# Sets of many short matmuls are kept four microseconds apart in the list schedule

## The chip, the cores and the metric

The kernel runs on one core of one Trainium2 chip. The metric is the device time of one execution in microseconds. The core's engines work side by side, each in the order of its own instruction queue: TensorE (PE) multiplies matrices, VectorE (DVE) and ScalarE (ACT) work elementwise and empty the PE's result banks, GpSimd (POOL) and SyncE (SP) issue transfers. A weight load (PEld in the profile) stands before every matmul in the PE's queue.

## The reference

For 2048 tokens with 512 channels the output is `g * a + (1 - g) * b`, where `g` is a sigmoid of a dot product of the token with `gate_w`.

- `a` is a state-space layer. For each channel a kernel `K` of length 2048 is summed from 128 complex exponentials, `K = 2 * einsum("dn,dnl->dl", C, P).real` with `P = exp(A * dt * l)`; the tokens are convolved with it over time (in the reference by an FFT of length 4096) and `u * D_skip` is added.
- `b` is a gated product without a nonlinearity: `h = (x @ w_gate) * (x @ w_up)`, then `h @ w_down`, with 1792 hidden columns.

All of it is float32.

## The kernel before

**The gated product.** Tokens, weights and `h` are each split into a high and a low float32 part, and each product is three matmuls of 128x128 by 128x512 (`THREE`: low weight, low token, both high). The 1792 hidden columns are 14 tiles in five groups, the tokens four chunks of 512; `hidden` makes one tile of `pg` and `pu` (eight products), `down` adds `h` into the output tiles `y`. 672 such products make 2016 large matmuls. The split tokens `xhi` and `xlo` are written to DRAM once (`x_d`) and read again, tile by tile through SP's queue, at each change of chunk. Weights come as `raw<-in_wts`.

**The convolution.** The channels go in 16 blocks of 32 (`k_block`) and, for the transforms, in four quarters of four blocks. DVE and ACT build two tables of powers, `x` and `v`, for a block; the PE multiplies them (`kgen`, 64 short matmuls into one bank `k`), and ACT moves the bank into `kt`. After four blocks `k_first` does the first Fourier stage of the kernel in two sets (8 and 24 matmuls). `transforms` then does the second stage (`m_second`, four sets of 64 matmuls from `in`, `w2s`), the product of the spectra on DVE (`m_product`), the inverse stage (`m_inverse`, two sets of 64 matmuls from `y`, `w3s`) and the last stage (`m_last`, two sets of four larger matmuls). Between the stages the data go through DRAM: `sk_d` and `su_d` into `m_second`, `y_d` into `m_last`. The short matmuls are plain float32 and work in parts of the array (`tile_position`). Each stands in the profile as two weight loads and two MATMUL records, so that a set of 64 is 128 MATMUL records. In the profile a `k<-v,x` set is `kgen`, `k<-in,w2s` (in the last quarter `k<-v,w2s` and `k<-x,w2s`) is `m_second`, and `k<-y,w3s` is `m_inverse`.

**What sets the order.** Nothing is issued directly. Every piece of work is a task with an engine, a duration in microseconds, what it reads and writes, and a rank, given to `add`. `Work.run` is a list scheduler: at each step it takes, over all engines, the task that can start first by its own account of time (then the lower rank), and notes its end. A product of the gated part has rank 2 and the convolution's sets have rank 1, 0 or -1, so a set goes ahead of the products as soon as its inputs are there, and the products fill the PE in between. The order that comes out is issued engine by engine (`InOrder` holds each engine to it), so the chip keeps the order but not the scheduler's times. The scheduler knows the durations and the number of buffers; it knows nothing of how instructions reach an engine. A set and a product stand in it like this:

```
add("pe", 0.681, fn, r=[...], w=[pg], rank=2, after=after)     # product: three large matmuls
add("pe", 2.15, kgen, r=[x, v], w=[pk], rank=0, hold=[kt])     # set of 64 short ones
```

All instructions are recorded by the one line L100 of a helper, so the profile's groups are told apart by the names of their tiles.

## Time and profile before

| | us |
|---|---|
| median of 3 runs | 633.33 (632.41 to 633.38) |
| the profiled execution | 631.22 |
| its span, from the first to the last instruction | 629.4 |
| PE busy in the span | 608.8 (97%) |
| DVE, ACT, POOL busy | 486.1, 397.0, 106.1 |
| DMA: bytes moved, mean rate | 142.63 MB, 227 GB/s |

The span is the time between the first and the last instruction of the profiled execution; 1.8 us of its 631.22 us lie around it. A view that names "issue" as the end of an idle time means that the engine waited for nothing that the profile shows: no other engine and no transfer of the kernel. Matmuls start before the ones ahead of them have ended, and their ends are modelled, so the spacing of the starts tells more than the busy time: large matmuls follow each other at 0.227 us, though each is given as 0.39 us long.

### The profile page before, as it was taken

What the parts mean: (1) busy time and instruction counts of PE and PEld (TensorE: products, weight loads), DVE (VectorE), ACT (ScalarE), POOL (GpSimd) and SP (SyncE); (2) the same over time, 40 slices, a digit from 0 to 9 for tenths busy, and PEclk for the clock granted to TensorE, in tenths of its full rate; (3) what the DMA queues carried; (4) which work ended last, traced back from release to release, by engine and by line L of the source; (5) the groups of instructions that cost most, each with busy time, mean ns of one, the idle gap of its engine ahead of it and who ended that gap; (6) DMA issues with size and microseconds to landing.
All of it is one profiled execution on the core that took longest, in us unless ns stands there. A gap on an engine that the chain in (4) does not pass through costs nothing.

```text
span 629.4 us, 17934 instructions
## 1 busy us (share of the span) xinstructions
PE 608.8 (97%) x7526; PEld 469.1 (75%) x7526; DVE 486.1 (77%) x760; ACT 397.0 (63%) x903; POOL 106.1 (17%) x157
## 2 busy tenths in 40 slices
PE   7899999999999999999999999999999998999997
PEld 5667768688687787877777887778787676786885
DVE  6858999999999898999999999899853255632113
ACT  5379778968787764887977687796544542222220
POOL 3143332211021110202110101201010030102210
PEclk9999999999999999999999999999999999999999
DMA  8899868557879697969998398899889598958841
GB/s 310 266 338 334 298 191 317 180 164 238 231 184 284 179 240 224 223 200 257 196 321 219 93 247 264 210 222 275 242 239 326 171 245 215 280 152 193 161 68 67
DMA packets 111892, 142.63 MB, mean 227 GB/s; under 512 B 7876, under 2 KB 66756, under 8 KB 111556
## 3 DMA queue, kind: packets, MB, share of 16 engines
q1 hardware_dynamic: 90100, 105.05, 52.9%
q0 software_dynamic: 21568, 36.45, 28.1%
q8 instruction: 59, 0.97, 0.6%
q14 instruction: 21, 0.17, 0.1%
q10 hardware_dynamic: 144, 0.00, 0.0%
HBM read 81.96 MB, written 59.51 MB: 225 GB/s over the span
## 4 chain that ended last, share of the span: by engine, by line
PE 89%; DMA 5%; issue 2%; DVE 2%; ACT 1%; SPq 0%; ACTq 0%; DVEq 0%
PE pu L100 23%; PE pg L100 23%; PE y L100 23%; PE k L100 20%; DMA raw<-in_xT 2%; DMA raw<-in_wts 2%; DMA xlo<-x_d 1%; DVE x L100 1%; DMA small<-in_rows 1%; DVE kt L100 0%; ACT ts L100 0%; ACT acc L100 0%; ACT xhi L100 0%; ACT dhi L100 0%; SPq L100 0%
## 5 line engine op out<-in xcount | busy, mean ns | idle before, releaser
L100 POOL DMA_DIRECT2D out<-acc x60 | 51.4, 901 | 357.9 <-ACT acc L100 333.1
L100 PE MATMUL pg<-xhi,wlo 128*128 128x512 f32 x224 | 89.7, 401 | 2.9 <-DVE wlo L100 1.8
L100 PE MATMUL y<-dhi,hl 128*128 128x512 f32 x224 | 89.7, 401 | 2.7 <-DVE hl L100 2.4
L100 PE MATMUL pu<-xhi,wlo 128*128 128x512 f32 x224 | 90.1, 402 | 0.4 <-issue 0.4
L100 PE MATMUL pg<-xlo,whi 128*128 128x512 f32 x224 | 87.9, 392 | 1.9 <-issue 1.2
L100 PE MATMUL pu<-xlo,whi 128*128 128x512 f32 x224 | 87.4, 390 | 0.0
L100 PE MATMUL y<-dhi,hh 128*128 128x512 f32 x224 | 87.4, 390 | 0.0
L100 PE MATMUL pg<-xhi,whi 128*128 128x512 f32 x224 | 87.3, 390 | 0.0
L100 PE MATMUL y<-dlo,hh 128*128 128x512 f32 x224 | 87.3, 390 | 0.0
L100 PE MATMUL pu<-xhi,whi 128*128 128x512 f32 x224 | 87.3, 390 | 0.0
L100 DVE TENSOR_TENSOR h<-pu,h 128x512 f32<-128x512 f32 x56 | 38.5, 688 | 59.4 <-PE pu L100 58.3
L100 ACT ACTIVATE acc<-y,ngate 128x512 f32<-128x512 f32 x76 | 52.1, 690 | 34.6 <-PE y L100 31.7
L100 ACT CAST hh<-h 128x512 fp32r<-128x512 f32 x56 | 34.7, 620 | 59.6 <-DVE h L100 59.6
L100 ACT COPY ts<-k 128x512 f32<-128x512 f32 (+1 forms) x116 | 48.8, 497 | 19.9 <-PE k L100 19.9
L100 ACT COPY h<-pg 128x512 f32<-128x512 f32 x56 | 32.9, 588 | 41.8 <-PE pg L100 37.5
L100 PEld LDWEIGHTS pg<-xhi,wlo 128*128 128x128 f32 x224 | 42.0, 188 | 19.4 <-issue 5.0
L100 PEld LDWEIGHTS y<-dhi,hl 128*128 128x128 f32 x224 | 42.0, 187 | 17.9 <-DVE hl L100 4.1
L100 PEld LDWEIGHTS pu<-xhi,wlo 128*128 128x128 f32 x224 | 42.0, 187 | 17.3 <-issue 8.3
L100 PEld LDWEIGHTS pg<-xlo,whi 128*128 128x128 f32 x224 | 42.1, 188 | 11.6 <-issue 1.6
L100 PEld LDWEIGHTS pu<-xhi,whi 128*128 128x128 f32 x224 | 42.1, 188 | 9.1
L100 PEld LDWEIGHTS y<-dhi,hh 128*128 128x128 f32 x224 | 42.0, 188 | 9.1
L100 PEld LDWEIGHTS pg<-xhi,whi 128*128 128x128 f32 x224 | 42.1, 188 | 9.0
(105 smaller groups left out, 1127.6 us busy)
## 6 DMA issues: line engine op xcount, KB each, us to landing
out<-acc POOLq DMA_DIRECT2D x60, 256.0 KB, 6.0
xhi<-x_d SPq DMA_DIRECT2D x48, 256.0 KB, 5.1
xlo<-x_d SPq DMA_DIRECT2D x48, 256.0 KB, 5.2
raw<-in_wts SPq DMA_DIRECT2D x36, 256.0 KB, 4.6
su_d<-ts POOLq DMA_DIRECT2D x32, 256.0 KB, 5.1
sk_d<-ts SPq DMA_DIRECT2D x16, 512.0 KB, 4.6
y_d<-ts SPq DMA_DIRECT2D x16, 512.0 KB, 5.7
in<-sk_d SPq DMA_DIRECT2D x12, 512.0 KB, 6.4
```

What stands on the lines that cost most here:

```text
L100: got = getattr(self.engine, name)(*args, **kw)
```

## The change

Each task gets a mark `many`, and the four kinds of set with the short matmuls carry it: `kgen`, both sets of `k_first`, `m_second` and `m_inverse` (48 sets in all; 40 of them have 64 matmuls). When the scheduler has placed such a task, no other one with the mark may start until 4.0 us after its end, by the scheduler's account. The sets of `u_part` and `m_last` don't carry the mark. Nothing is computed differently, and no task is added or removed.

```
@@ class Work:
+    APART = 4.0
...
-    def add(self, engine, us, fn, r=(), w=(), rank=1, after=0.0, dma=0, hold=(), rows=()):
+    def add(self, engine, us, fn, r=(), w=(), rank=1, after=0.0, dma=0, hold=(), rows=(), many=False):
...
-        task.rows = rows
+        task.rows, task.many = rows, many
@@ def run(self):
-        bus, order, known, rows = 0.0, [], {}, {}
+        bus, order, known, rows, apart = 0.0, [], {}, {}, 0.0
...
-                start = max([at, free[t.engine]] + [rows[r] for r in t.rows if r in rows])
+                start = max([at, free[t.engine], apart * t.many] + [rows[r] for r in t.rows if r in rows])
...
             left[t.engine].remove(t)
+            if t.many:
+                apart = start + t.us + self.APART
@@ k_block, k_first, m_second, m_inverse
-        add("pe", 2.15, kgen, r=[x, v], w=[pk], rank=0, hold=[kt])
+        add("pe", 2.15, kgen, r=[x, v], w=[pk], rank=0, hold=[kt], many=True)
...
-            add("pe", 2.08, fn, r=[kt, m_w1k], w=banks, rank=-1, hold=sts)
+            add("pe", 2.08, fn, r=[kt, m_w1k], w=banks, rank=-1, hold=sts, many=True)
...
-        add("pe", 2.13, fn, r=[*ins, w], w=banks[0] + banks[1], rank=1, hold=tos)
+        add("pe", 2.13, fn, r=[*ins, w], w=banks[0] + banks[1], rank=1, hold=tos, many=True)
...
-        add("pe", 2.13, fn, r=[*ys, *ws], w=banks, rank=1, hold=sts)
+        add("pe", 2.13, fn, r=[*ys, *ws], w=banks, rank=1, hold=sts, many=True)
```

What it moves shows in the built programs. Up to the fifth `kgen` set (the first of the second quarter) the PE's queues are the same. There, on the PE, the last short matmul of `k_first` (`k<-kt,w1k_t`) and the set stood like this before:

```order
L100 MATMUL k_2144<-kt_1007,w1k_t_89 128x128
L100 MATMUL pu_2054<-xhi_2020,wlo_1338 128x512
L100 MATMUL pu_2054<-xlo_2025,whi_1334 128x512
L100 MATMUL pu_2054<-xhi_2020,whi_1334 128x512
L100 MATMUL pg_2187<-xhi_1754,wlo_1417 128x512
L100 MATMUL pg_2187<-xlo_1762,whi_1406 128x512
L100 MATMUL pg_2187<-xhi_1754,whi_1406 128x512
L100 MATMUL pg_2187<-xhi_1992,wlo_1417 128x512
L100 MATMUL pg_2187<-xlo_1997,whi_1406 128x512
L100 MATMUL pg_2187<-xhi_1992,whi_1406 128x512
L100 MATMUL k_2201<-v_639,x_1674 32x64 x64
```

and now end like this:

```order
L100 MATMUL pg_2187<-xhi_2000,wlo_1417 128x512
L100 MATMUL pg_2187<-xlo_2006,whi_1406 128x512
L100 MATMUL pg_2187<-xhi_2000,whi_1406 128x512
L100 MATMUL pg_2187<-xhi_2020,wlo_1417 128x512
L100 MATMUL pg_2187<-xlo_2025,whi_1406 128x512
L100 MATMUL pg_2187<-xhi_2020,whi_1406 128x512
L100 MATMUL pu_2214<-xhi_1754,wlo_1417 128x512
L100 MATMUL pu_2214<-xlo_1762,whi_1406 128x512
L100 MATMUL pu_2214<-xhi_1754,whi_1406 128x512
L100 MATMUL k_2219<-v_639,x_1674 32x64 x64
```

The nine large matmuls of the first listing stand ahead of these nine as before, so the set has 18 large matmuls between itself and the set before it, where it had nine. The same happens along the rest of the queue. Of the 47 gaps between marked sets, 15 held fewer than 18 large matmuls before (6, 9, 12 or 15), and two held exactly 18. Now none holds fewer, and 23 hold exactly 18. Sets also change places: before, `m_inverse`, a `kgen` and an `m_second` followed each other with six large matmuls in each gap; now the `kgen` goes ahead of the `m_inverse`.

The other engines' queues follow. On SP, in the third quarter, the stores of the inverse stage (`y_d<-ts`) and the loads for the last stage (`in<-y_d`) stood before ahead of stores of the next quarter's `k_first` and of weight loads:

```order
L100 DMA y_d_59<-ts_6683 128x8x128
L100 DMA y_d_59<-ts_6708 128x8x128
L100 DMA x_6803<-su_d_57 128x8x128 x2
L100 DMA sk_d_58<-ts_6831 128x1024
L100 DMA in_6851<-y_d_59 128x2x512
L100 DMA in_6856<-y_d_59 128x2x512
L100 DMA in_6858<-y_d_59 128x2x512
L100 DMA sk_d_58<-ts_6840 128x1024
L100 DMA raw_6883<-in_wts 128x512
```

and now stand in the middle of the token tiles' reload at a change of chunk:

```order
L100 DMA y_d_59<-ts_7169 128x8x128
L100 DMA y_d_59<-ts_7181 128x8x128
L100 DMA w2s_7284<-in_w2 128x512
L100 DMA xhi_7389<-x_d_60 128x512
L100 DMA xlo_7392<-x_d_60 128x512
L100 DMA in_7394<-y_d_59 128x2x512
L100 DMA in_7396<-y_d_59 128x2x512
L100 DMA in_7401<-y_d_59 128x2x512
L100 DMA xhi_7412<-x_d_60 128x512
L100 DMA xlo_7419<-x_d_60 128x512
```

One pair of `xhi` and `xlo` is now issued ahead of the three `in<-y_d`, and the other three pairs behind them.

## The prediction

> **What bounds the kernel now.** I read the page first: busy shares, the queue of instruction transfers, the shares of the chain that ended last.

> ```profile
> PE 608.8 (97%) x7526; PEld 469.1 (75%) x7526; DVE 486.1 (77%) x760; ACT 397.0 (63%) x903; POOL 106.1 (17%) x157
> ...
> q8 instruction: 59, 0.97, 0.6%
> ...
> PE 89%; DMA 5%; issue 2%; DVE 2%; ACT 1%; SPq 0%; ACTq 0%; DVEq 0%
> ```

> The PE is the bound: 97% busy, 89% of the chain. So an edit that moves no work can gain only what the PE loses between its instructions. "issue", 2% of 629.4 us, is the largest such loss after the transfers of the start: 9 to 16 us by the rounding. Second, the PE's waits:

> ```profile
> PE k L100 <- issue: 7.0, 8, 1.9
> PE y L100 <- DVE hl L100: 2.4, 1, 2.4
> ...
> PE pg L100 <- issue: 1.2, 1, 1.2
> ...
> PE pg L100 <- DMA xlo<-x_d: 0.4, 1, 0.4
> ```

> Eight waits of 7.0 us together lie inside the sets of short matmuls (`k`) and end for no reason that the kernel gives. Third, the chain of waits from 500 to 552 us (start, length, what), where four sets in a row are touched:

> ```profile
> 509.55 2.04 PE k L100 x120
> ...
> 512.03 1.66 PE pu L100 x6
> ...
> 517.10 1.69 PE k L100 x105
> 518.80 1.88 issue
> 520.68 0.63 PE k L100 x22
> 521.31 2.26 PE pu L100 x9
> ...
> 526.30 2.72 PE pu L100 x12
> 529.02 2.02 PE k L100 x125
> 531.04 2.26 PE y L100 x9
> 533.30 1.07 PE k L100 x63
> 534.37 0.85 issue
> 535.23 1.16 PE k L100 x65
> 536.38 2.27 PE y L100 x9
> 538.65 0.68 PE pg L100 x3
> 539.33 1.36 PE y L100 x6
> 540.69 0.83 PE k L100 x45
> 541.52 0.10 issue
> 541.62 1.50 PE k L100 x82
> 543.12 2.96 PE y L100 x12
> ```

> An undisturbed set takes 2.02 us (529.02 to 531.04); the four others take 2.48, 4.21, 3.08 and 2.43. Where they break tells why. From 535.23 to the break at 541.52 the PE issues 65 short, 18 large and 45 short matmuls: 128, with their weight loads 256 instructions. The page has 15,052 PE instructions (7526 and 7526) and 59 packets of instructions: 255 for each packet. So the PE stops at the edge of a block of code, one packet long. A set of 128 records is just such a block and is gone in 2 us; large matmuls at 0.227 us (12 in 2.72) use up a block in 29 us. The window from 518.3 to 519.4 us has this row on that queue:

> ```profile
> q8 instruction: 1, 0.02, 5.4%
> ```

> 5.4% of 16 engines over 1.1 us is 0.95 us for one packet. It moves while the PE stands (from 518.80), and the PE goes on at 520.68, at least 1.3 us behind it. The next code is simply late, and the other engines have no part in it. A second piece of the chain, from 230 to 246 us, shows sets close together:

> ```profile
> 236.84 1.26 PE k L100 x69
> ...
> 238.12 1.09 PE k L100 x52
> 239.21 1.60 PE pg L100 x6
> 240.81 1.21 PE k L100 x66
> 242.02 1.18 issue
> 243.19 1.13 PE k L100 x61
> 244.32 1.83 PE pu L100 x7
> ```

> With 1.6 us of other work between them the two sets take 2.37 and 3.51 us.

> **The change part by part.**

> *Removed: the waits for code.* What they cost is the excess of a set over 2.02 us, more than the wait itself, since a wait is counted from a modelled end: 2.19 against 1.88, 1.06 against 0.85, 1.49 against 1.18, on average 0.28 more. The eight waits thus cost 7.0 + 8 x 0.28 = 9.2 us. Three smaller ones that this list doesn't give (the sets at 236.84, 509.55 and 540.69: 0.35, 0.46, 0.41) add 1.2. Together **10.5 us**, rounded up for a few tenths in sets that I don't quote. The 1.2 us before a `pg` lies ahead of the first row that the change moves and stays.

> *What spacing leaves of it.* The gap that the new order guarantees is 18 large matmuls, 4.08 us. With the set and some 0.2 us at its edges that is 6.3 us from set to set, carrying 146 matmuls; the edge of a block returns after 128, so 0.28 us of a set earlier: every 6.0 us. How long does a late PE wait for its next block? From resumption to resumption one block on: 238.12 to 243.19, 5.07 us; 535.23 to 541.62, 6.39; 512.03 to 520.68, 8.65. Against 6.0 us the first is harmless, the others are too long by 0.4 and 2.65. Low bound of what stays: nothing, as in the set at 529.02 with 7.7 us of other work ahead. High bound: the mean overshoot of these three, 1.0 us, in each of the 23 gaps of exactly 18, 23 us; but these are the worst of 59 packets, and most sets are clean even now. I take it that slow packets come as often as now and meet a tight stretch as often: 0.4 + 2.65 = **3.0 us** stay.

> *Added: edges.* A set between large matmuls costs some 0.2 us more than the sum of its parts: from its end to the last of six large ones, 239.21 to 240.81, pass 1.60 us where six at 0.227 are 1.36. The scheduler's new order leaves one set and the two last `m_last` no longer side by side: 2 x 0.2 = **0.4 us**.

> *Moved: sets come up to 4 us later against the products.* Behind each stand ACT's copies out of the bank, and DVE's next table `v`, for which there is one buffer; on DVE the `h` and `hl` of the gated product stand in the same queue. The cover is the PE's own stock of products: it loses time only when it reaches a product whose `hl` or token is late. How thin is DVE?

> ```profile
> 320.00:400.00 80.00, 78.60 (x1260) 62.62 (x1241) 76.88 (x111) 57.59 (x129) 9.85 (x12) 1.00 0.81 219
> ...
> 480.00:560.00 80.00, 76.72 (x1080) 59.33 (x1079) 39.84 (x59) 31.40 (x64) 10.09 (x10) 1.00 0.87 233
> ```

> The third busy time is DVE's: 76.9 of 80 us, later 39.8. Its chain of tables may slip by a few microseconds in the middle and has the room of the last stage to end in. If that cover went, each microsecond that DVE lags would be one of the PE's. The tokens' reload is thin as well (the page's row of its transfers, and a piece of the chain):

> ```profile
> xhi<-x_d SPq DMA_DIRECT2D x48, 256.0 KB, 5.1
> ```

> ```profile
> 384.99 6.49 DMA xlo<-x_d
> ...
> 391.52 0.73 PE pg L100 x2
> ```

> One slow `xlo` is on the chain there, though by the list of waits it cost the PE 0.4 us. Bounds for new waits: below zero (a shifted order may miss even this one, -0.4), above some 5 us, twelve reloads (48 tiles, four at a time) at 0.4 each. I take **0.5 us**, nearer to the present rows.

> *Sum.* 10.5 - 3.0 - 0.4 - 0.5 = 6.6 us. From the profiled execution, 631.22 us, that leaves 624.6 (span 622.8). The median of the runs shown is 633.33, 2.1 us above the profiled one; for runs of that kind I predict **626.7 us**.

> [...]

> **The rivals.**

> *Four microseconds are too few.* For it: the set at 517.10 has 5.07 us of large matmuls ahead and loses 2.19 us, the one at 540.69 has 4.3 us ahead and loses 0.41. [...] Against it: the two lost most where one packet took 8.65 us. Then half of 10.5 is left: 633.3 - 5.2 + 0.9 + some 0.6 of later sets = 629.6.

> *The gain is handed back.* The PE, no longer held up, runs into DVE at 77 of 80 us and into DMA reloads, and waits there as long: 633.3, within 1 us. For it: both are thin. Against it: no wait of the PE for DVE is longer than 2.4 us, and that one lies at the start. If the idle time isn't code at all and the sets keep it wherever they stand, only the edges are added: 633.3 + 0.4 = 633.7. [...] Against it stands the break after 128 pairs with the packet in it; 0.03 for it, 0.08 for the first.

> *SP's queue holds up the tokens (slower).* In the third quarter three of four token pairs now stand behind the three `in<-y_d`, which must wait for the two `y_d` stores just ahead to land. The view of the transfers of `y_d` has:

> ```profile
> DMA to landing us min/median/max: 4.0/6.0/10.6
> ```

> A store of 10.6 us and a reload of 6.5 us behind it are 17 us until those tokens are there. The PE covers part of it, with the 18 matmuls of a gap and two sets (8 us) at least; 9 us would be lost: 633.3 - 6.6 + 9 = 635.7. It decides once the tokens come more than 6.6 us late. At the median of 6.0 us the cover is enough, which is why I hold it unlikely.

> **How the numbers follow.** Forecast 0.61, spacing too short 0.20, handed back 0.08, not code 0.03, tokens held up 0.08. The forecast's own bounds: all 10.5 us and the xlo wait gone, less 0.4 of edges, is 10.5 us less, 622.8; as a profile like that of 631.22 may also come out among the runs, the range begins a little lower, at 621.5. Above it takes in the too short spacing with its uncertainty of some 2 us: 631.5. About 0.2 are left out, the other three cases. The first two cases are faster by more than 0.2% (1.3 us, about what a measurement of this kernel can tell from no change): 0.81; the next two are within it: 0.11; the last is slower: 0.08.

> **What would show it.** Right: the waits `PE k <- issue` fall from 7.0 us to 2 or 3, no set takes over 3 us but one or two, the share of "issue" in the chain is 1%, PE busy stays near 609 us in a span of 623. The sets still break where 128 pairs have passed since the last break. Wrong on spacing: the waits stay above 4 us, in sets with 18 large matmuls ahead. Wrong on cover: `PE pg <- DMA xlo<-x_d` or `PE y <- DVE hl` grow to several microseconds. The whole reading falls if `PE k <- issue` stays at 7 us while the order on the PE is the new one.

## The result and the profile after

The median went from 633.84 us (631.65 to 637.11, 20 runs) to 629.74 us (624.31 to 634.32, 20 runs), 4.1 us less. The ratio of the two kernels' times is 0.9924 with an interval of 0.9904 to 0.9944, which is 4.8 us less (3.5 to 6.1). One run here (634.32 us) and one of 1210.92 us in an experiment below stand well above the others of their kernel and are left out of the ratios. The forecast was 626.7 us. The time lies within its range and 3.0 us above its number.

The profiled execution of the changed kernel took 630.77 us, hardly less than the 631.22 us of the one before. Its page, the busy times, the queue of instruction transfers and the shares of the chain that ended last:

```profile
PE 611.9 (97%) x7526; PEld 471.6 (75%) x7526; DVE 486.6 (77%) x760; ACT 398.1 (63%) x903; POOL 106.2 (17%) x157
...
q8 instruction: 59, 0.97, 0.6%
...
PE 92%; DMA 4%; DVE 2%; issue 1%; ACT 0%; SPq 0%; ACTq 0%
```

The share of "issue" has halved, but the PE, with the same instructions, is busy for 3.1 us more (before: 608.8). The list of the PE's waits (us in total, times, longest):

```profile
PE k L100 <- issue: 3.7, 3, 1.8
PE y L100 <- DVE hl L100: 3.0, 1, 3.0
...
PE pg L100 <- ACT h L100: 1.7, 2, 1.3
PE pg L100 <- issue: 1.4, 1, 1.4
```

The waits inside the sets fell from 7.0 us in eight to 3.7 in three. The wait for `xlo<-x_d` isn't there any more, and no other wait for a transfer stands in its place. The chain of waits from 500 to 552 us, the piece that the prediction showed of before:

```profile
505.86 2.02 PE k L100 x125
...
510.83 0.91 PE pu L100 x4
511.74 0.22 issue
511.96 0.63 PE pu L100 x2
512.59 1.94 PE k L100 x124
514.53 1.80 issue
516.34 0.40 PE k L100 x2
516.74 2.00 PE pu L100 x6
518.74 3.93 PE pg L100 x12
...
523.35 1.99 PE k L100 x127
...
529.64 2.02 PE k L100 x125
...
542.39 2.72 PE pg L100 x12
...
546.47 2.02 PE k L100 x125
```

Where four of six sets lost time before, one of seven does now: it breaks two records before its end and loses over 2 us. Behind it 12 large `pg` matmuls take 3.93 us, where 12 take 2.72 further on. The PE's timeline shows why (start, length, what; rows between left out):

```profile
517.47 0.41 PE L100 MATMUL pu<-xhi,wlo 128*128 128x512 f32 x1
...
518.53 0.63 PE L100 MATMUL pg<-xhi,wlo 128*128 128x512 f32 x1
518.96 0.63 PE L100 MATMUL pg<-xlo,whi 128*128 128x512 f32 x1
...
521.35 0.39 PE L100 MATMUL pg<-xlo,whi 128*128 128x512 f32 x1
521.57 0.39 PE L100 MATMUL pg<-xhi,whi 128*128 128x512 f32 x1
```

The starts are 0.43 us apart instead of 0.22: for 3.41 us the granted clock is half, and about 1.7 us are lost. The trace has another such stretch of 6.83 us from 22.8 us on; it begins in the 3.0 us wait for `hl` (20.7 to 23.7 us) that stands, with 2.4 us, at the same place before. Before had none; its mean granted clock is 1.000, this one's 0.990.

An account by the starts of the matmuls, for the two profiled executions: the first `kgen` set starts 3.67 us later although nothing ahead of it on the PE has moved (that clock, and the waits of the start). From there to the end the changed kernel takes 4.08 us less: the sets' excess over an undisturbed set fell from 11.9 to 5.9 us, 6.0 less, and the products, the half clock among them, took 1.9 more.

### The profile page after: what moved, and what is told of

It reads as the page before. It is cut to its first block, busy times and chain, and to the rows that moved or that the text cites. A ratio compares the mean times of both kernels' runs of the same rounds, so it can differ in the third digit from the quotient of the medians.

```text
span 629.0 us, 17946 instructions
## 1 busy us (share of the span) xinstructions
PE 611.9 (97%) x7526; PEld 471.6 (75%) x7526; DVE 486.6 (77%) x760; ACT 398.1 (63%) x903; POOL 106.2 (17%) x157
## 4 chain that ended last, share of the span: by engine, by line
PE 92%; DMA 4%; DVE 2%; issue 1%; ACT 0%; SPq 0%; ACTq 0%
PE pg L100 24%; PE pu L100 24%; PE y L100 24%; PE k L100 20%; DMA raw<-in_wts 2%; DMA raw<-in_xT 1%; DMA small<-in_rows 1%; DVE x L100 0%; DVE v L100 0%; DVE kt L100 0%; DVE h L100 0%; SPq L100 0%; DVE hl L100 0%; ACT acc L100 0%; DVE y L100 0%
## 5 line engine op out<-in xcount | busy, mean ns | idle before, releaser
L100 POOL DMA_DIRECT2D out<-acc x60 | 51.5, 902 | 363.4 <-ACT acc L100 333.6
L100 PE MATMUL pg<-xhi,wlo 128*128 128x512 f32 x224 | 91.4, 408 | 2.7 <-ACT h L100 1.7
L100 PE MATMUL y<-dhi,hl 128*128 128x512 f32 x224 | 89.9, 402 | 3.1 <-DVE hl L100 3.0
L100 PE MATMUL pg<-xlo,whi 128*128 128x512 f32 x224 | 88.9, 397 | 1.7 <-issue 1.4
L100 PE MATMUL pu<-xhi,wlo 128*128 128x512 f32 x224 | 90.0, 402 | 0.0
L100 PE MATMUL pg<-xhi,whi 128*128 128x512 f32 x224 | 88.5, 395 | 0.0
L100 PE MATMUL pu<-xlo,whi 128*128 128x512 f32 x224 | 87.5, 391 | 0.2 <-issue 0.2
L100 PE MATMUL y<-dhi,hh 128*128 128x512 f32 x224 | 87.6, 391 | 0.0
L100 PE MATMUL pu<-xhi,whi 128*128 128x512 f32 x224 | 87.6, 391 | 0.0
L100 PE MATMUL y<-dlo,hh 128*128 128x512 f32 x224 | 87.6, 391 | 0.0
L100 DVE TENSOR_TENSOR h<-pu,h 128x512 f32<-128x512 f32 x56 | 38.6, 689 | 47.9 <-PE pu L100 46.9
L100 ACT ACTIVATE acc<-y,ngate 128x512 f32<-128x512 f32 x76 | 51.9, 688 | 32.9 <-PE y L100 28.3
L100 ACT CAST hh<-h 128x512 fp32r<-128x512 f32 x56 | 34.7, 620 | 51.2 <-DVE h L100 50.9
L100 ACT COPY ts<-k 128x512 f32<-128x512 f32 (+1 forms) x116 | 48.8, 501 | 23.8 <-PE k L100 23.7
L100 PEld LDWEIGHTS pg<-xhi,wlo 128*128 128x128 f32 x224 | 42.9, 191 | 23.0 <-issue 5.6
L100 ACT COPY h<-pg 128x512 f32<-128x512 f32 x56 | 33.0, 588 | 39.6 <-PE pg L100 36.0
L100 PEld LDWEIGHTS y<-dhi,hl 128*128 128x128 f32 x224 | 42.1, 188 | 18.1 <-DVE hl L100 4.5
L100 PEld LDWEIGHTS pu<-xhi,wlo 128*128 128x128 f32 x224 | 42.0, 187 | 15.1 <-issue 5.9
L100 PEld LDWEIGHTS pg<-xlo,whi 128*128 128x128 f32 x224 | 42.8, 191 | 11.3 <-issue 1.8
L100 PEld LDWEIGHTS pg<-xhi,whi 128*128 128x128 f32 x224 | 42.8, 191 | 9.3
L100 PEld LDWEIGHTS pu<-xhi,whi 128*128 128x128 f32 x224 | 42.2, 188 | 9.4 <-issue 0.4
L100 PEld LDWEIGHTS y<-dhi,hh 128*128 128x128 f32 x224 | 42.2, 188 | 9.2
## 6 DMA issues: line engine op xcount, KB each, us to landing
out<-acc POOLq DMA_DIRECT2D x60, 256.0 KB, 6.3
xhi<-x_d SPq DMA_DIRECT2D x48, 256.0 KB, 5.4
xlo<-x_d SPq DMA_DIRECT2D x48, 256.0 KB, 5.7
raw<-in_wts SPq DMA_DIRECT2D x36, 256.0 KB, 3.0
su_d<-ts POOLq DMA_DIRECT2D x32, 256.0 KB, 5.0
```

The costliest lines, as they stand in the source:

```text
L100: got = getattr(self.engine, name)(*args, **kw)
```

## The experiments

The theory: late blocks of code cost the time, and the spacing gives each block time to come. Its rivals: four microseconds are too few; what counts is not the distance but where the edges of the blocks happen to fall; the order gains or loses something that has nothing to do with code. Each ratio is against the kernel before on the same chip.

**The changed kernel again**, for a second profile.

> The changed kernel once more, to see how its waits and its clock vary. Code theory (the gain is the shorter wait for blocks of code): the waits PE k <- issue are 2 to 5 us again, against 7.0 in the profile of before, and the ratio to the kernel before is 0.990 to 0.994. Clock theory (half of the expected gain is eaten by stretches at half clock, which a PE wait of about 3 us at the first y product brings on): where the granted clock of a run is 1.00 the time is 624 to 627, where it is 0.99 it is 629 to 632. Chance theory (the new order happens to fit this kernel's other waits better): nothing new to expect.

Measured: 628.12 us, ratio 0.9904 (0.988 to 0.9928). The set at 313.5 us lost 1.9 us and the one at 508.5 us 2.4. They are the two that lost most in the first profile (at 316.2 and 512.5 us): the places repeat. The stretch at half clock behind the wait for `hl` did not, though that wait was 3.0 us again.

**Two microseconds apart, and five.**

```
-    APART = 4.0
+    APART = 2.0        # the other kernel: 5.0
```

> The spacing is 2.0 us instead of 4.0: at least nine large matmuls (2.04 us) between marked sets, 16 gaps hold fewer than 18. Code theory: the edge of a block returns after some 4.1 us, less than the 5 to 8 us that a late block takes, so most of the waits are there as before: PE k <- issue 5 to 8 us, time 0 to 1.5 us under the kernel before. Chance theory: a time that bears no relation to the gaps; it may be as good as with 4.0.

> The spacing is 5.0 us: at least 24 large matmuls (5.4 us) in each gap. Code theory: the edge of a block returns after 7.4 us or more; PE k <- issue falls to 0 to 2 us, and the time falls 1 to 3 us under that of the changed kernel, if the sets' later places don't starve the PE; if they do, new waits on DVE or DMA appear late in the program and eat it. Chance theory: no such fall of the waits inside sets.

Two microseconds lost time, where 0 to 1.5 us less than before had been expected: 638.03 us, ratio 1.0053 (1.0028 to 1.0078), with as many waits in sets as before, but longer ones:

```profile
PE k L100 <- issue: 10.6, 8, 2.6
```

Five took every wait for code out of the sets; their one long wait is for a transfer:

```profile
PE k L100 <- DMA in<-su_d: 1.6, 1, 1.6
PE pg L100 <- issue: 1.5, 1, 1.5
```

Yet it took 628.64 us, ratio 0.9911 (0.9886 to 0.9936), no better than four. Its PE ends earlier, at 618.8 us (621.5 in the second profile with four), but the tail grew. The end of its chain of waits:

```profile
609.79 0.76 DVE kt L100
...
611.56 3.58 PE k L100 x16
615.14 3.64 PE y L100 x15
...
618.81 0.76 DVE kt L100
```

The sets came so late that the last `m_last` (16 records) stands almost at the end, and 7.4 us of DVE work and stores follow the last matmul, 4.0 with four microseconds apart.

**`k_first` without the mark.**

```
-            add("pe", 2.08, fn, r=[kt, m_w1k], w=banks, rank=-1, hold=sts, many=True)
+            add("pe", 2.08, fn, r=[kt, m_w1k], w=banks, rank=-1, hold=sts)
```

> The mark is taken off the two sets of k_first alone, which have 16 and 48 MATMUL records, not 128. Code theory: these sets use up a small part of a block each, so the waits stay as in the changed kernel (2 to 5 us) and the time is within 1.5 us of it. A theory by which every change of matmul shape costs the wait would have them return: 1 to 2 us longer.

Measured: 627.41 us, ratio 0.9892 (0.9849 to 0.9934), not to be told from the changed kernel; 3.8 us of waits in four sets.

**Few instructions in the sets.** In both orders the 40 sets of 64 matmuls become four large matmuls each, of about the same time; the convolution's true products are left out. `m_second`, as an example:

```
-                for part in range(2):
-                    for i in range(2):
-                        for j in range(4):
-                            for e in range(2):
...
+                for e in range(2):
+                    half = slice(64 * e, 64 * e + 64)
+                    pe.matmul(
+                        banks[which][e].t, w.t[half, 0:2, :].rearrange("p a b -> p (a b)"),
+                        src.t[half, k, 0:4, :].rearrange("p a b -> p (a b)"), start=True, stop=True,
+                        tile_position=(64 * e, 0),
+                    )
```

> The kernel before, in its own order, with the 40 sets of 64 short matmuls (kgen, m_second, m_inverse) each replaced by four large ones on the same tiles: 8 MATMUL records instead of 128, so a thirtieth of the code. It leaves out the convolution's true products (the output is not the reference's); all copies, transfers and waits stay. Four such matmuls take 1.87 to 1.92 us in the rows of u_part and m_last, so the sets themselves save 16 x 0.13 + 24 x 0.09 = 4.2 us. Code theory: the waits PE k <- issue vanish (under 0.5 us), and the time falls by 4.2 and another 10 to 12 us: 618 to 620. If the idle time were not code (a wait for banks, for copies, for tokens), it would stay in that order: 629 to 630.

> The same replacement in the order of the changed kernel. Code theory: with little code to fetch the spacing has nothing left to save, so it is as long as few_before, or up to 1.5 us longer by its edges and its later sets: 618 to 621. Chance theory (the new order is better by itself, code or no code): still 4 to 6 us shorter than few_before.

In the order of before: 613.86 us, ratio 0.967 (0.9646 to 0.9694). Of its pages the queue of instructions, and all waits of its PE over 1 us:

```profile
q8 instruction: 21, 0.34, 0.2%
```

```profile
PE y L100 <- DVE hl L100: 2.9, 2, 1.8
PE pg L100 <- DVE wlo L100: 1.7, 1, 1.7
PE k L100 <- DVE acc L100: 1.5, 1, 1.5
```

With 21 packets instead of 59 no wait for "issue" is left, though the order, the inputs, the buffers and the transfers of data are those of before. The short matmuls are gone as well as their code; that it is the count of instructions that matters, the next experiment shows. 21 us are gone, 4 of them the sets' own time (the new sets take less than undisturbed old ones), so some 17 us are left for code and whatever else the short matmuls bring; 11.9 of them are the sets' waits by the starts.

In the changed order the same kernel took 616.92 us, ratio 0.9709 (0.9678 to 0.974), 3 us more. Most of that lies ahead of the first moved instruction: its first `kgen` set starts at 86.8 us, at 84.0 in the other, and only its trace has a stretch at half clock before that, 3.41 us from 24.7 us on. From there to the start of the last matmul it takes 523.8 us against 523.1. So the order by itself, where code isn't late, costs about 0.7 us and gains nothing.

**The edges of the blocks moved.** The three matmuls of `warm` at the start are cut into four pieces each, in both kernels, so that every edge falls 18 matmul records earlier in the program:

```
             for _ in range(3):
-                pe.matmul(scratch.t, zero.t[:, :P], zero.t, start=True, stop=True)
+                for n in range(4):
+                    part = slice(P * n, P * n + P)
+                    pe.matmul(scratch.t[:, part], zero.t[:, :P], zero.t[:, part], start=True, stop=True)
```

> The kernel before, with its three warming matmuls of 512 columns at the start each cut into four of 128: 9 more matmuls, which are 18 more MATMUL records and 18 more weight loads, ahead of everything else. Code theory: the sets break where a fixed count of PE instructions has passed, so each break lies 18 matmuls earlier in its set or in the set before: the one near 204 us, which breaks after 46 of 128 matmuls, breaks after 28; the one near 241 us after 48 instead of 66; the one near 518 us after some 88 instead of 106. If data or banks caused the wait, the breaks would stay at 46, 66 and 106. The time may differ by a few microseconds either way, since other sets are hit.

> The changed kernel with the same cut of the warming matmuls, so that its blocks of code begin 18 matmuls earlier. Spacing theory (the gap itself protects the sets): the time is that of the changed kernel within 2 us (626 to 631), since 18 large matmuls stand in each gap wherever the edges fall; the moved edges cost the kernel before 7 us. Alignment theory (the change gained because its edges happen to fall well): as far from the changed kernel as the shifted kernel before is from its own, 633 to 636.

The set at 204 us broke after 46 records in the kernel before:

```profile
204.19 0.92 PE L100 MATMUL k<-in,w2s 64*32 64x128 f32 x46
206.62 1.49 PE L100 MATMUL k<-in,w2s 64*32 64x128 f32 x82 [1.51 <-issue]
```

and with the edges moved by 18 it breaks after 28:

```profile
206.08 0.65 PE L100 MATMUL k<-in,w2s 64*32 64x128 f32 x28
208.15 1.74 PE L100 MATMUL k<-in,w2s 64*32 64x128 f32 x100 [1.42 <-issue]
```

The break follows the count of instructions, as foretold. The second one foretold came too (at 245.42 us, after 49 records where 48 were expected); the set of the third was not broken. The time did not stay: 641.59 us, ratio 1.0108 (1.0058 to 1.0158) for the order of before, from two runs that lie 6 us apart, and 633.91 us, ratio 0.9967 (0.9938 to 0.9996), for the changed one. The first lost 1.1%, 7 us, and the second 0.4%, 3 us, for nothing but the edges. 633.91 us lies in the range that the alignment theory had named, 633 to 636. With pieces of 64 columns the edges move by 42 records:

```
-                for n in range(4):
-                    part = slice(P * n, P * n + P)
+                for n in range(8):
+                    part = slice(64 * n, 64 * n + 64)
```

> The kernel before with its warming matmuls cut into eight of 64 columns each: the edges lie 42 matmuls earlier than in the kernel before. Both theories: a break near 206 us after 46 - 42 = 4 of 128 matmuls, or the edge lies so early in the set that the queue ahead of it hides it. Spacing theory: 632 to 642 us, never as short as the changed kernel at its three places of the edges. Alignment theory: any time from 626 to 642.

> The changed kernel with edges 42 matmuls earlier. Spacing theory: 626 to 631 us and waits PE k <- issue of 2 to 5 us for a third time, several microseconds under the kernel before with the same shift. Alignment theory: no closer to the other two places than the kernels before are to each other.

642.7 us, ratio 1.012 (1.0075 to 1.0165), and 636.05 us, ratio 1.0033 (1.0003 to 1.0063). So at three placements of the edges the spacing saves 0.8, 1.4 and 0.9% (differences of the ratios; 5 to 9 us), and the placement, with the order held, is worth 0.4 to 1.2%, as much. With 42 not all of that is the edges: in those two profiles the clock rises to full only at 15.4 and 15.7 us (4.6 to 7.6 us in the other twelve), and the first `kgen` set starts at 88.3 and 88.9 us (83.6 to 87.2). The sets' excess by the starts leaves the beginning out: some 14 us in the order of before and 10 in the changed one with 18, 13 and 10 with 42, against 11.9 and 5.9 with the edges in their first places. The expected 626 to 631 us of the spacing theory was missed twice. The PE's waits in the changed order with 42:

```profile
PE k L100 <- issue: 7.7, 4, 4.2
```

**Work in the wait for `hl`.** Eight large matmuls whose result nobody reads go ahead of the third product of the first `y`:

```
     def down(y, r, h, w, first, last, fill=()):
         def fn():
+            for _ in range(8 if fill else 0):
+                pe.matmul(scratch[0].t, fill[0].t[:, :P], fill[1].t, start=True, stop=True)
```

> The changed kernel with eight extra large matmuls (1.8 us, into an unused bank) in the PE's wait of 3 us ahead of the third y product, at 20 to 24 us. Clock theory: the stretch at half clock that follows this wait in four of six profiles no longer comes; the mean clock of the runs is 0.997 to 1.000 and the time 1 to 2 us under that of the changed kernel. If the wait isn't what lowers the clock, the clock and the time stay as they were.

The place in the changed kernel, and with the eight matmuls (`k<-xhi,whi`):

```profile
23.69 0.79 PE L100 MATMUL y<-dhi,hl 128*128 128x512 f32 x1 [2.96 <-DVE hl L100]
24.28 0.63 PE L100 MATMUL y<-dlo,hh 128*128 128x512 f32 x1
```

```profile
20.49 1.97 PE L100 MATMUL k<-xhi,whi 128*128 128x512 f32 x8
23.66 0.50 PE L100 MATMUL y<-dhi,hl 128*128 128x512 f32 x1 [1.20 <-DVE hl L100]
23.99 0.39 PE L100 MATMUL y<-dlo,hh 128*128 128x512 f32 x1
```

The PE goes on at the same time, but at full clock. Measured: 626.61 us, ratio 0.9866 (0.9838 to 0.9894), the lowest of all that compute the whole result; the mean granted clock of its six runs was 0.995 to 1.000, in the changed kernel's twenty 0.989 to 1.000. The profile has no stretch at half clock ahead of the last matmul. But the eight matmuls also move every later edge by eight records, so how much of the gain is the clock's isn't shown; the waits in its sets came to 4.0 us, 3.7 in the changed kernel.

**All together**: 4.5 us apart (at least 21 large matmuls between sets), no mark on `k_first`, and the eight matmuls.

```
-    APART = 4.0
+    APART = 4.5
```

> A version put together from the runs: spacing 4.5 us (21 large matmuls), no mark on k_first, and the eight filling matmuls in the wait at 20 us. Code theory: the edge of a block returns after 6.7 us, so PE k <- issue is 0 to 2 us; the time is 621 to 625 us, 1 to 4 us under the changed kernel with the filling alone. If the later last stage of the convolution lengthens the end, as with a spacing of 5.0, the time is 625 to 628.

Missed: 629.76 us, ratio 0.9932 (0.9899 to 0.9966), no better than the changed kernel. One set accounts for much of it. The chain of waits ahead of it, and the PE's timeline at it:

```profile
396.03 1.58 PE pu L100 x6
397.61 2.72 PE pg L100 x12
400.33 2.72 PE pu L100 x12
403.05 2.04 PE pg L100 x9
```

```profile
404.70 0.39 PE L100 MATMUL pg<-xhi,whi 128*128 128x512 f32 x1
405.02 2.04 PE L100 MATMUL k<-v,x 128*32 128x64 f32 x127
411.20 0.31 PE L100 MATMUL k<-v,x 128*32 128x64 f32 x1 [4.14 <-issue]
```

It has 39 large matmuls, 9 us, between itself and the set before it, and still waits 4.14 us. Distance alone does not protect it.

**What a block lasts.** This set shows more of what decides. It breaks after 127 records; the edge before lies 128 records back, one large matmul ahead of the set. The whole block is the set, and it is gone in 2.1 us, whatever stands ahead of the edge. I counted the PE's instructions of twelve traces off in blocks of 256, from 90 to 575 us, and set the time in which each block is issued against the wait at its end (the longest distance between two starts there, counted from 0.45 us):

| | blocks issued in under 5 us, of them late | blocks of 5 us and more, of them late |
|---|---|---|
| before, two apart, both shifts of before | 63, 33 | 149, 9 |
| the changed kernel (two profiles) and six variants of it | 70, 29 | 353, 11 |

| kernel | short blocks | late | these waits, us | longest, us |
|---|---|---|---|---|
| before | 16 | 8 | 8.6 | 1.78 |
| two apart | 16 | 9 | 12.7 | 2.91 |
| before, edges moved by 18 / 42 | 17 / 14 | 8 / 8 | 14.0 / 14.9 | 3.17 / 3.34 |
| changed | 7 | 3 | 5.6 | 2.07 |
| changed, edges moved by 18 / 42 | 7 / 10 | 5 / 5 | 10.2 / 9.8 | 3.22 / 4.42 |
| five apart | 10 | 1 | 1.9 | 1.93 |
| all together | 9 | 3 | 7.8 | 4.36 |

About every second block that is used up in under 5 us is followed by a late one; of the longer ones one in 25. Two of those twenty waits are over 2 us (before at 520.68 us, 2.15; two apart at 468.7 us, 2.39), and both stand behind a block that had itself begun late. Spacing halves the number of short blocks, from some 16 to 7 to 10. It cannot end them: 128 records of a set and 18 of products make 146, so the edges walk through the sets and now and then fall just ahead of one. Five apart has as many short blocks as the others and was late at one; with other placements of the edges it wasn't tried.

The packets on the instruction queue, whose times stand in the traces, tell the late blocks from the others. From 90 to 575 us the twelve traces have 64 pauses of over 0.3 us that are put down to "issue". All lie at an edge of the count of 256, to within an instruction, and each ends 1.2 to 1.7 us after the end of a packet of code: in the set above the packet ends at 409.67 us and the PE goes on at 411.20. Where a short block was followed by a late one, that packet had started 3.0 us after the beginning of the short block (median), where it wasn't, 0.4 us. With five apart it came by 0.4 us in nine of ten cases. What makes a packet start as late as 3.7 us (that set) or 6.3 us (before, the block from 512.03 us on) stays open.

## Why the prediction came out as it did

**The cause held.** The waits in sets are late code: the breaks follow the count of instructions to within a record, the PE goes on 1.2 to 1.7 us behind the end of a packet of code, and with 21 packets instead of 59 the waits vanish. The rival that the idle time isn't code falls.

**The waits removed** were taken as 10.5 us in sets; by the starts 11.9 us, over the same sets. Near enough.

**What spacing leaves of it is the step that failed.** I took 3.0 us; the profiles have 5.9 and 5.0, and 6.3 without the mark on `k_first`. My working said that with 18 large matmuls the edge returns every 6.0 us. Of the 53 blocks from 90 to 575 us of the changed kernel's profile 17 do last 6.0 to 6.2 us, and only one of these is late, by 0.22 us. Sixteen of the 17 begin with an edge inside a set. When it falls among the large matmuls, as it does ahead of six of that profile's seven short blocks, the next block is those few and almost a whole set, and lasts 2.3 to 4 us. The set at 512.5 us is one: its 62 + 64 records and two large ones. I had written that a set of 128 records is just such a block and gone in 2 us, and did not apply it to the new order. The price of such a block was underrated as well: the longest wait of before was 1.9 us, and the runs have waits of up to 4.2 us. With the edges moved, some 10 us stayed in the sets.

**Edges added**: 0.4 us predicted, 0.7 us by the pair with few instructions. With these sizes the sum is 11.9 - 5.9 - 0.7 = 5.3 us, within the measured 3.5 to 6.1.

**New waits**: 0.5 us predicted, none found; `xlo<-x_d` went from 0.4 us to nothing. SP's order, with three `in<-y_d` ahead of the tokens, cost nothing, so the rival that ends slower falls, and so does the one in which DVE or the reloads take the gain back.

**A term was missing**: half clock behind a wait. In the changed kernel's profile 3.41 us of it follow the wait of 1.80 us at 514.5 us, and 6.83 us come with the wait of 2.96 us at 20.7 us; at half speed 1.7 and 3.4 us are lost. The profiled execution of before, on which the whole sum rests, had none of them; 45 of that kernel's 52 runs in the last section have a mean clock of 0.997 or less. One stretch would also be the larger part of the 2.1 us by which its median lies above that execution. But the term stands on both sides of the comparison, and only its difference counts: the mean granted clock was 0.995 over the changed kernel's twenty runs and 0.996 over 52 of the kernel before, a difference of some 0.7 us by the unrounded means (an estimate).

**The first rival** gave 629.6 us, with half of the waits left. Its number and its half came true; its reason did so only in part. The set that lost most does stand behind a block that was itself late: at 511.96 us the PE had waited 0.22 us among the products just ahead of it. In the profile of before one of ten late blocks stands so, that of the set at 517.10 us. But more distance is no cure, as 39 large matmuls ahead of a wait of 4.14 us show. So the spacing gained by making short blocks fewer, not by making them impossible. That the time lies in the forecast's range, and so near to this rival's number, is partly luck: with the edges elsewhere the same order took 633.91 and 636.05 us, above the range's 631.5.

The signs that I had named: `PE k <- issue` fell to 3.7 us, between "2 or 3" and the "above 4" that would have spoken against the spacing; "issue" fell to 1% of the chain; the span did not fall to 623 us, because of the half clock, and in the second profile of the same kernel it was 625.5.

## What to carry to other kernels

Where the profile shows idle time in the middle of a run of short instructions, ended by nothing, count the instructions back to the last such break: if the distance is a whole number of blocks (256 instructions here, at all 64 pauses), late code is the first suspect. Then look at how long each block lasts rather than at how far the dense pieces lie apart: here 62 of 133 blocks issued in under 5 us were followed by a late one and 20 of 502 longer ones, and a dense piece as long as a block makes a short one wherever an edge falls just ahead of it. Fewer instructions per piece took the cause away (8 records instead of 128 left no wait for "issue"). And before a sum is made against one profiled execution, its granted clock is compared with that of the timed runs (1.000 against a mean of 0.996 here). All these numbers are this kernel's; no other was measured.

## What the runs showed of the hardware that I had not expected

```profile
PE k L100 <- issue: 6.6, 4, 3.0
PE y L100 <- DVE hl L100: 3.0, 1, 3.0
```

**The placement of code was worth 0.4 to 1.2%.** Twelve or 24 small matmuls for three large ones at the start, in work that is otherwise the same, made both kernels slower by 0.4 to 1.2% (3 to 8 us; with 24, part of it is the later clock). So two edits of the number of PE instructions ahead of the dense pieces moved the time by as much as this change did (0.8%); what makes one packet of code start late and another not stays open.
